# One loop of 64 attention steps over two batches, with both merges at the end, in a Branchformer forward-and-backward kernel

## The chip, the cores and the metric

The kernel runs on one core of a Trainium2 chip. The metric is the device time of one execution in microseconds. A core has a matrix engine (TensorE, in the profile PE, with its weight loads as PEld), three engines for elementwise work (VectorE: DVE, ScalarE: ACT, GpSimd: POOL) and a sequencer (SyncE: SP) that here only issues DMA transfers. Each engine works through its own queue in order; semaphores tie them together. SBUF is the core's memory of 128 partitions, PSUM the banks into which PE writes.

## The reference

The inputs are x of shape (2, 4000, 144) in bf16, weights, and grad_out of x's shape. Cut to what is computed, the forward function is

```python
xa = layernorm(x)
q, k, v = split(xa @ w_qkv, 3)
p = softmax(q @ k.T * D ** -0.5)                     # 4000 x 4000 per batch
glob = (p @ v) @ w_att_out
u, g = split(gelu(xa @ w_mlp_in), 2)
g = layernorm(g)
gc = sum(pad(g)[i:i+T] * dw_csgu[i] for i in range(5))
loc = (u * gc) @ w_mlp_out
m = concat(glob, loc)
m = m + sum(pad(m)[i:i+T] * dw_merge[i] for i in range(5))
y = x + m @ w_merge
```

and the kernel returns y together with the vector-Jacobian product for grad_out: the gradient of x and of all seven weights (nine outputs).

## The kernel before

A batch's 4000 tokens are laid out as 125 partitions of 32 tokens, token number 32 p + j in partition p, column j. So a "tile" or "block" j of the 32 is one token of each partition, 125 tokens in all (PB = 125, NB = 32). The normalised input xa_aug holds xa in this layout with a column of ones; xaT_m and R hold its transpose (128 channels and the remaining 16), XR the remaining channels stacked for four matmuls at once, goT the transposed grad_out. acc (125 x 32 x 144, f32) collects the gradient of xa for all blocks, and Yn_d, ug_d and Zn_d are DRAM tensors for per-tile results.

The attention of a batch, `phase_att` (from L1029), is a loop over the 32 query tiles with a drain behind it. The steps are software-pipelined. In step t:

- `jit_mm` and `jit_tr` (L1069, L1090) project the queries and the upstream gradients of tile t + 1 and transpose them.
- `quad` (L1107, L1113) multiplies them with all 4000 keys into PSUM tiles ps, 1000 columns each: scores S of tile t and dP of tile t - 1, four of each in a step.
- `S_min` (L1130, DVE) takes S from PSUM into Pbuf with the running minimum, `P_exp` (L1137, ACT) makes P from it, `PdP` (L1145 directly on DVE, or L1147 on ACT and L1149 on DVE) takes dP and multiplies it with P into Sbuf.
- `P_tr` (L1140) and `st_half` (L1311) have the DMA transpose P into PT and P*dP, in two halves, into ST. Both are issued by SP.
- `Y_half` (L1157) sums PT times xa_aug over the 32 blocks, `Z_half` (L1195) ST times xa_aug; the results are scaled (L1163 to L1179, L1199) and stored to Yn_d and Zn_d.
- `X_group` (L1234) sums, for three blocks of the keys, the products with Sbuf and Pbuf of the last two tiles in PSUM, and a DVE add (L1240; L1238 for the first write) brings them into acc. In each step half of the blocks are served, the even or the odd ones.

Between these, `local_units` (L421) gives the local branch, forward and backward, in small units that are dealt out evenly over the steps: over steps 2 to 30 in batch 0 and over steps 0 to 30 in batch 1.

The order of the instructions in this loop is not that of the source. `Planner.plan` (L784) takes the recorded instructions from step 2 of a batch to the end of its loop, simulates them with a table of costs per engine and DMA, and fixes an order on each engine. Outside of the loop, the Tile framework orders the instructions and the waits, buffers being shared through pools of tiles with a fixed number of slots. SP's and Pool's queues are in order in both.

Behind the loop of a batch stands its merge, the class `Merge` (L1429). `open_early` loads grad_out (go_h), the attention and local results (Yg) and the matrices VU through Pool's queue, behind a gate on the last ST; `Hmm` (L1502) forms the products H of grad_out's five shifts with those results (the gradients of the merge), 12 matmuls for each of 32 blocks; `tr_pieces` (L1420, L1425 with ACT copies L1421, L1426) transposes the results into YT and YS; `dm1` (L1559) forms Zn times xa; `out_g` (L1581, L1583, DVE add of x L1584) gives y for four blocks, eight times; `dx_a` (L1593, L1596) and `dx_b` (L1603, L1607, ACT L1608, POOL L1610) turn acc into the gradient of x. H of batch 0 is copied out of PSUM (L1546), stored to DRAM and added to that of batch 1 (L1548).

The main function (from L1800) runs: a head that prepares weights and batch 0; attention of batch 0; merge 0, with the preparation of batch 1 (`pre_pieces`, L337: layernorm statistics L361, normalisation L384, transposes L349 to L396) dealt out between its pieces; attention of batch 1, which begins with memsets and zero loads of Pbuf's and Sbuf's pads (L1047, L1048); merge 1 together with the weight gradients (`Final`, L1618 on). Both batches use the same tiles xaT_m, R, XR, goT and acc.

Of the kernel before, what the change touches and what calls it, by code (L numbers as in the profile page):

```python
# [7 lines left out]
BF = mybir.dt.bfloat16  # L8
# [297 lines left out]
def pre_tiles(k, b, S, xp, gp, sp):  # L306

    nc = k.nc
    NB = k.NB
    S.x_tp = xp.tile([PB, NB, D], BF, name="x_tp%d" % b)  # L310
    S.go_q = gp.tile([PB, NB + 6, D], BF, name="go_q%d" % b)
    ln_tiles(k, b, S, sp)
# [102 lines left out]

G2 = 2
# [3 lines left out]

def local_units(k, W, b, S, A, es, DHT, ps_w):  # L421

# [3 lines left out]
    pl = es.enter_context(tc.tile_pool(name="loc%d" % b, bufs=1, side="right", reuse_waits="tile"))  # L426
    sm = es.enter_context(tc.tile_pool(name="loc_sm%d" % b, bufs=4, side="right", reuse_waits="tile"))
# [155 lines left out]
    def dhT_unit(g):  # L583
        pt = ps_w.tile([96, 3 * G2, 128], BF, tag="w")
        dh = dhr[g % 2]
        for bi in range(G2):
            for ct in range(3):
                nc.tensor.transpose(pt[:, 3 * bi + ct, 0:PB], dh[:, bi, ct * 96:(ct + 1) * 96], W.ident[0:PB, 0:PB])
        dhT = sm.tile([96, 3 * G2, PB], BF, tag="dhT", bufs=3)
# [76 lines left out]
class Planner:  # L666
# [117 lines left out]
    def plan(self, i0, i1, window=400):  # L784
# [234 lines left out]
        self.groups, self.order, self.times = groups, order, times  # L1019
# [9 lines left out]
def phase_att(k, W, b, S, A, M, head=None):  # L1029
    nc, tc = k.nc, k.tc  # L1030
    NB, NG, T = k.NB, k.NG, k.T
    NCH = NG
# [3 lines left out]
    with ExitStack() as es:  # L1036
        ab = es.enter_context(tc.tile_pool(name="att_buf%d" % b, bufs=1, side="left", reuse_waits="tile"))
        small = es.enter_context(tc.tile_pool(name="att_small%d" % b, bufs=4, side="left", reuse_waits="tile"))
        gw = es.enter_context(tc.tile_pool(name="att_gw%d" % b, bufs=3, side="left", reuse_waits="tile"))
        ps_sg = es_sg.enter_context(tc.tile_pool(name="ps_sg%d" % b, bufs=2, space=PSUM, side="right", reuse_waits="tile"))  # L1040
        ps_yz, ps_w = k.ps_yz, k.ps_w
        Pbuf = ab.tile([128, NPB, GW], BF, name="Pbuf")
        Sbuf = ab.tile([128, NDB, GW], BF, name="Sbuf")
        def pads():
            for (buf_, nb_) in ((Pbuf, NPB), (Sbuf, NDB)):
                for n_ in range(nb_):
                    nc.gpsimd.dma_start(buf_[PB:128, n_, :], k.zdram[0:128 - PB, :])  # L1047
                nc.gpsimd.memset(buf_[0:PB, :, :].rearrange("p n (a b) -> p (n a) b", b=128)[:, :, PB:128], 0.0)  # L1048
        PT = ab.tile([128, NB, 128], BF, name="PT")
        ST = ab.tile([128, NB, 128], BF, name="ST")  # L1050
        QBs = ab.tile([PB, NPB, 2, D], BF, name="QBs")
        qbr = [ab.tile([PB, 2, D], BF, name="qb%d" % i) for i in range(3)]
        qrr = [ab.tile([PB, 256], BF, name="qr%d" % i) for i in range(3)]
        znr = [ab.tile([PB, 256], BF, name="zn%d" % i) for i in range(2)]
        def clr():
            for t_ in qrr:
                nc.gpsimd.memset(t_[:], 0.0)
            for t_ in znr:
                nc.gpsimd.memset(t_[:, D:256], 0.0)
        if head is None:  # L1060
            clr()
        xaTm, R, XR, xaa = S.xaT_m, S.R, S.XR, S.xa_aug
        QT, QB, RL, TY, YZ, ZN, ZT, NM, DHT = {}, {}, {}, {}, {}, {}, {}, {}, {}
        units, u0 = [], (0 if head is None else 2)
        if head is None:
            pads()
            units += local_units(k, W, b, S, A, es_loc, DHT, ps_w)

        def jit_mm(i):  # L1069
            ti = slice(i * PB, (i + 1) * PB)  # L1070
            pj = ps_w.tile([PB, 2 * D], F32, tag="w")
            nc.tensor.matmul(pj[:], R[:, ti], W.RW[:, 0:2 * D], start=True, stop=False)
            nc.tensor.matmul(pj[:, 0:D], xaTm[:, ti], W.Q0[:], start=False, stop=False)
            for kk in range(5):
                h = i + 4 - kk
                nc.tensor.matmul(pj[:, D:2 * D], S.goT[:, h * PB:(h + 1) * PB], W.VUT[:, kk, 0:D], start=False, stop=(kk == 4))
            qb = qbr[i % 3]
            nc.scalar.copy(qb[:], pj[:].rearrange("p (a b) -> p a b", b=D))
            QB[i] = qb
            for h in range(2):  # L1080
                rems(nc.gpsimd.tensor_copy, i, h)

        def rems(eng, i, h):


            v = qrr[i % 3][:].rearrange("p (a r c) -> p a r c", a=4, r=2)
            v = v[:, 0:4:3, :, 0:DR] if h == 0 else v[:, 1:3, :, 0:DR]
            eng(v, QB[i][:, h, 128:D].rearrange("p (a r c) -> p a r c", a=1, r=1).to_broadcast([PB, 2, 2, DR]))

        def jit_tr(i):  # L1090
            qb = QB[i]
            pt = ps_w.tile([128, 4, 128], BF, tag="w")
            for q, src in enumerate((qb[:, 0, 0:128], qrr[i % 3][:, 0:128], qrr[i % 3][:, 128:256], qb[:, 1, 0:128])):
                nc.tensor.transpose(pt[:, q, 0:PB], src, W.ident[0:PB, 0:PB])
            qt = gw.tile([128, 4, PB], BF, tag="qt")
            nc.scalar.copy(qt[:], pt[:, :, 0:PB])
            QT[i] = qt

        def pchunk(pb, c2):
            return Pbuf[0:PB, pb, c2 * 1024:(c2 + 1) * 1024]  # L1100

        def quad(work, stacked=True):


            pp = [ps_sg.tile([PB, 2, 512], F32, tag="sg", name="ps") for _ in range(len(work) // 2)]
            for r, (i, h, c) in enumerate(work):
                mm = nc.tensor.matmul(pp[r // 2][:, r % 2, 0:CH], QT[i][:, 3 * h, :], xaTm[:, c * CH:(c + 1) * CH], start=True, stop=False)  # L1107
            with tc.issue_after(mm.ins):
                for r, (i, h, c) in enumerate(work):
                    q = c % 4 if stacked else 3  # L1110
                    rs = slice(32 * q, 32 * q + DR)
                    xr = XR[rs, (c // 4) * CH:(c // 4 + 1) * CH] if stacked else R[rs, c * CH:(c + 1) * CH]
                    nc.tensor.matmul(pp[r // 2][:, r % 2, 0:CH], QT[i][rs, 1 + (q // 2 + h) % 2, :], xr, start=False, stop=True)  # L1113
            return [p[:, :, 0:CH].rearrange("p h (a b) -> p h a b", b=PB) for p in pp]

        def S_work(i, c2):
            return [(i, 0, 2 * c2), (i, 0, 2 * c2 + 1)]

        def dP_work(i, c2):
            return [(i, 1, 2 * c2), (i, 1, 2 * c2 + 1)]  # L1120

        def pv(buf, n, c2):
            return buf[0:PB, n, c2 * 1024:(c2 + 1) * 1024].rearrange("p (h a b) -> p h a b", h=2, b=128)[:, :, :, 0:PB]

        def S_min(i, c2, src):

            if c2 == 0:
                NM[i] = small.tile([PB, 5], F32, tag="nm", name="nm")
            if True:
                nc.vector.tensor_scalar(pv(Pbuf, i % NPB, c2), src, -1.0, 3.0e38, op0=ALU.mult, op1=ALU.min, accum_out=NM[i][:, c2:c2 + 1])  # L1130
            if c2 == 3:
                nc.vector.tensor_reduce(NM[i][:, 4:5], NM[i][:, 0:4], axis=AX.X, op=ALU.min)  # L1132

        def P_exp(i, c2):

            v = pv(Pbuf, i % NPB, c2)
            nc.scalar.activation(v, v, ACT.Exp, bias=NM[i][:, 4:5], scale=-1.0)  # L1137

        def P_tr(i):
            nc.sync.dma_start_transpose(out=PT[:], in_=Pbuf[:, i % NPB, :])  # L1140

        def PdP(i, c2, src, direct):

            if direct:
                nc.vector.tensor_tensor(pv(Sbuf, i % NDB, c2), src, pv(Pbuf, i % NPB, c2), op=ALU.mult)  # L1145
            else:
                nc.scalar.copy(pv(Sbuf, i % NDB, c2), src)  # L1147
                sc = Sbuf[0:PB, i % NDB, c2 * 1024:(c2 + 1) * 1024]
                nc.vector.tensor_tensor(sc, sc, pchunk(i % NPB, c2), op=ALU.mult)  # L1149

        def Y_half(i, h):
            if h == 0 and i not in YZ:
                yz = ps_yz.tile([PB, 2, 145], F32, tag="yz")
                YZ[i] = yz
            Y = YZ[i][:, 0, :]
            for j in range(16 * h, 16 * h + 16):
                nc.tensor.matmul(Y, PT[0:PB, j, 0:PB], xaa[:, j, 0:D + 1], start=(j == 0), stop=(j == NB - 1))  # L1157
# [871 lines left out]
```

## Time and profile before

| | us |
|---|---|
| time, median of 3 runs | 1391.16 |
| lowest and highest of the runs | 1387.9, 1392.22 |
| the profiled execution's own time | 1390.59 |
| its span in the trace | 1388.8 |
| first S_min of tile 3, batch 0 | 80.4 |
| first S_min of tile 31, batch 0 | 585.2 |
| first S_min of tile 0, batch 1 | 719.8 |
| first S_min of tile 2, batch 1 | 746.4 |
| first S_min of tile 31, batch 1 | 1258.5 |
| last add into acc, batch 1 | ends about 1310 |

The span is what the trace holds of one execution; the rest of the execution's own time lies around it. All times of the profile are counted from the start of the span. The times of the first S_min of a tile mark the pace of the loop: 28 steps from 80.4 to 585.2 are 18.03 us each, 29 steps from 746.4 to 1258.5 are 17.66 us each.

### The profile page before, as it was taken

How to read it: one execution, taken by the hardware profiler on the slowest of the kernel's cores; microseconds unless marked ns; L12 is line 12 of the kernel's file. 1: busy time of each engine (PE TensorE's matmuls, PEld its weight loads, DVE VectorE, ACT ScalarE, POOL GpSimd, SP SyncE). 2: the span in 40 equal slices, each digit the busy share in tenths (PEclk: the TensorE clock that was granted, in tenths of full speed). 3: DMA queues.
4: the chain of work that ended last, by engine and by line, in shares of the span. 5: the costliest groups of instructions: out<-in, count | busy, mean ns of one | idle time of the engine just before them, and what ended most of it. 6: DMA issues, size and time to landing. Idle time of an engine off the chain costs nothing.

```text
span 1388.8 us, 39713 instructions
## 1 busy us (share of the span) xinstructions
PE 1290.7 (93%) x16254; PEld 1067.0 (77%) x16254; DVE 1055.4 (76%) x2815; ACT 830.3 (60%) x1387; POOL 539.3 (39%) x1087
## 2 busy tenths in 40 slices
PE   5989999999999999989887999999999999999898
PEld 3677777778877877879765778788887787778797
DVE  6578888788887877758647888788888887877564
ACT  5856665666666666634526656666766665665271
POOL 8534333334334342256424334343443433334320
PEclk9999999999999999999999999999999999999999
DMA  4467857677767767784217677877776766767512
GB/s 118 90 121 139 145 105 126 114 132 128 121 127 130 121 119 131 111 186 121 85 44 124 127 127 130 130 130 135 126 139 123 134 125 124 142 124 148 140 43 72
DMA packets 553637, 168.59 MB, mean 121 GB/s; under 512 B 536432, under 2 KB 548354, under 8 KB 553413
## 3 DMA queue, kind: packets, MB, share of 16 engines
q1 hardware_dynamic: 547818, 153.74, 60.5%
q0 software_dynamic: 5088, 12.11, 3.4%
q8 instruction: 127, 2.08, 0.6%
q14 instruction: 56, 0.45, 0.1%
q10 hardware_dynamic: 548, 0.21, 0.1%
HBM read 21.04 MB, written 14.12 MB: 25 GB/s over the span
## 4 chain that ended last, share of the span: by engine, by line
PE 44%; DMA 7%; DVE 7%; ACT 4%; POOL 2%; issue 2%; DVEq 0%; SPq 0%; POOLq 0%; ACTq 0%
PE X L1234 10%; PE ps L1107 8%; PE yz L1195 5%; PE yz L1157 5%; DMA PT<-Pbuf 3%; PE ps L1113 3%; PE po L1581 3%; DMA go_h<-in_grad_out_dram 1%; DVE t L1607 1%; DMA ST<-Sbuf 1%; DVE Pbuf L1130 1%; ACT Pbuf L1137 1%; PE pd L564 1%; DVE acc L1240 1%; PE pc L549 1%
## 5 line engine op out<-in xcount | busy, mean ns | idle before, releaser
L1130 DVE TENSOR_SCALAR_CACHE_REDUCE Pbuf<-ps 125x1000 bf16<-125x1000 f32 x256 | 306.6, 1199 | 115.3 <-PE ps L1113 110.9
L1137 ACT ACTIVATE Pbuf<-Pbuf,nm 125x1000 bf16<-125x1000 bf16 x256 | 282.9, 1135 | 126.0 <-DVE nm L1132 125.7
L1234 PE MATMUL X<-QBs,Sbuf 125*125 125x144 bf16 x2048 | 304.3, 230 | 4.7 <-DVE acc L1240 2.8
L1234 PE MATMUL X<-QBs,Pbuf 125*125 125x144 bf16 x2048 | 300.1, 228 | 4.0 <-POOL QBs L1179 4.0
L1234 PEld LDWEIGHTS <-Sbuf 125*125 125x125 bf16 x2048 | 264.9, 139 | 20.0 <-issue 19.9
L1107 PE MATMUL ps<-xaT_m,qt 128*125 128x500 bf16 x1024 | 264.6, 377 | 9.8 <-DVE Pbuf L1130 4.1
L1147 ACT CAST Sbuf<-ps 125x1000 bf16<-125x1000 f32 x189 | 187.9, 994 | 138.4 <-PE ps L1113 137.9
L1234 PEld LDWEIGHTS <-Pbuf 125*125 125x125 bf16 x2048 | 265.6, 139 | 5.8 <-issue 5.3
L1240 DVE TENSOR_TENSOR acc<-X,acc 125x432 f32<-125x432 f32 x372 | 202.0, 551 | 54.9 <-PE X L1234 53.4
L1195 PE MATMUL yz<-xa_aug,ST 125*125 125x144 bf16 x2048 | 150.6, 229 | 20.9 <-ACT ty L1173 19.9
L1195 PEld LDWEIGHTS <-ST 125*125 125x125 bf16 x2048 | 141.5, 139 | 27.5 <-issue 26.0
L1107 PEld LDWEIGHTS <-qt 128*125 128x125 bf16 x1024 | 121.7, 137 | 52.7 <-issue 13.7
L1157 PE MATMUL yz<-xa_aug,PT 125*125 125x145 bf16 x2048 | 147.1, 230 | 8.6 <-DMA PT<-Pbuf 8.1
L1149 DVE TENSOR_TENSOR Sbuf<-Sbuf,Pbuf 125x1024 bf16<-125x1024 bf16 x189 | 133.9, 709 | 23.0 <-ACT Sbuf L1147 22.8
L1157 PEld LDWEIGHTS <-PT 125*125 125x125 bf16 x2048 | 137.8, 139 | 16.2 <-DMA PT<-Pbuf 11.9
L1113 PEld LDWEIGHTS <-qt 16*125 16x125 bf16 x1024 | 37.0, 128 | 100.5 <-issue 99.9
L1113 PE MATMUL ps<-XR,qt 16*125 16x500 bf16 x1016 | 113.8, 422 | 0.0
L1145 DVE TENSOR_TENSOR Sbuf<-ps,Pbuf 125x1000 bf16<-125x1000 f32 x67 | 80.0, 1194 | 5.2 <-PE ps L1113 4.0
L597 POOL TENSOR_TENSOR A_dwc<-l_fl,A_dwc 128x512 f32<-128x512 f32 (+2 forms) x48 | 35.6, 741 | 103.0 <-ACT l_fl L596 103.0
L1175 POOL TENSOR_SCALAR QBs<-qb,rl 125x144 bf16<-125x144 bf16 x64 | 25.4, 397 | 127.5 <-DVE rl L1163 121.2
L1209 ACT COPY zt<-pt 128x250 bf16<-128x250 bf16 x64 | 23.7, 371 | 69.3 <-PE pt L1207 69.1
L574 POOL TENSOR_SCALAR l_w<-gd,nc,c 125x144 f32<-125x144 bf16 x64 | 30.6, 486 | 85.5 <-DVE nm L1132 44.7
(557 smaller groups left out, 2557.4 us busy)
## 6 DMA issues: line engine op xcount, KB each, us to landing
Yn_d<-yn SPq DMA_DIRECT2D x64, 35.2 KB
Zn_d<-zn SPq DMA_DIRECT2D x64, 35.2 KB
ug_d<-ugr SPq DMA_DIRECT2D x32, 70.3 KB
xo<-in_x_dram SPq DMA_DIRECT2D x16, 140.6 KB
out_dram<-dxo SPq DMA_DIRECT2D x16, 140.6 KB
go_h<-in_grad_out_dram POOLq DMA_DIRECT2D x4, 504.0 KB, 7.1
Zn<-Zn_d SPq DMA_DIRECT2D x4, 504.0 KB
ST<-Sbuf SPq DMA_TRANSPOSE x124
```

Source lines behind the costliest of these rows:

```text
L1107: mm = nc.tensor.matmul(pp[r // 2][:, r % 2, 0:CH], QT[i][:, 3 * h, :], xaTm[:, c * CH:(c + 1) * CH], start=True, stop=False)
L1113: nc.tensor.matmul(pp[r // 2][:, r % 2, 0:CH], QT[i][rs, 1 + (q // 2 + h) % 2, :], xr, start=False, stop=True)
L1130: nc.vector.tensor_scalar(pv(Pbuf, i % NPB, c2), src, -1.0, 3.0e38, op0=ALU.mult, op1=ALU.min, accum_out=NM[i][:, c2:c2 + 1])
L1137: nc.scalar.activation(v, v, ACT.Exp, bias=NM[i][:, 4:5], scale=-1.0)
L1145: nc.vector.tensor_tensor(pv(Sbuf, i % NDB, c2), src, pv(Pbuf, i % NPB, c2), op=ALU.mult)
L1147: nc.scalar.copy(pv(Sbuf, i % NDB, c2), src)
L1149: nc.vector.tensor_tensor(sc, sc, pchunk(i % NPB, c2), op=ALU.mult)
L1157: nc.tensor.matmul(Y, PT[0:PB, j, 0:PB], xaa[:, j, 0:D + 1], start=(j == 0), stop=(j == NB - 1))
L1195: nc.tensor.matmul(Z, ST[0:PB, j, 0:PB], xaa[:, j, 0:D], start=(j == 0), stop=(j == NB - 1))
L1234: nc.tensor.matmul(X[:, jj, :], l, r, start=(n_ == 0), stop=(n_ == len(ops) - 1))
L1240: nc.vector.tensor_tensor(av, X[:, 0:nj, :], av, op=ALU.add)
L1581: nc.tensor.matmul(po[:, q, :], YT[h][:, (i + kk) * PB:(i + kk + 1) * PB], VU[h][:, kk, :], start=(n_ == 0), stop=False)
```

## The change

The loop of `phase_att` runs over s = 0 to 64 for both batches; tile s belongs to batch s // 32. Pipelining goes on across the seam: in step 32, S is of batch 1's first tile and dP of batch 0's last. The planner now takes everything from step 2 to behind the drain as one piece. Local units of batch 0 are dealt out over steps 2 to 27, those of batch 1 over steps 34 to 61.

Batch 1 gets tiles of its own for xa_aug, xaT_m, R, XR and goT; acc stays one tile. In steps 28 to 31 the new function `prep_late` prepares batch 1, in 30 pieces that are dealt out evenly: x and grad_out come in four groups of 8 tokens, each in one buffer, on SP's queue.

```diff
+def prep_late(k, W, b, S, es, pst):
...
+    def load(Q, v, n, g):
+        if g < 4:
+            Q[g] = sp.tile([PB, 8, D], BF, tag=n, name=n, bufs=1)
+            load_tok(k, Q[g], 0, v, 8 * g, 8 * g + 8, nc.sync)
...
+    def stats(g):
+        for j in range(8):
+            nc.vector.bn_stats(st[:, 8 * g + j, :], XQ[g][:, j, :])
...
+    def norm(g):
...
+        for j in range(8 * g, 8 * g + 8):
+            eng = nc.vector if j % 2 else nc.gpsimd
+            eng.tensor_scalar(S.xa_aug[:, j, 0:D], XQ[g][:, j % 8, :], S.rstd_x[:, j:j + 1], nmr[:, j:j + 1], op0=ALU.mult, op1=ALU.add)
...
+    P = [lambda: (start(), load(XQ, xv, "xq", 0), load(GQ, gv, "gq", 0)), halos]
+    for g in range(4):
+        P += [lambda g=g: stats(g), lambda g=g: gr(g), lambda g=g: (norm(g), load(XQ, xv, "xq", g + 1)), lambda g=g: (gm(2 + 8 * g, GQ[g][:]), load(GQ, gv, "gq", g + 1))]
+        if g:
+            P += [lambda g=g: gs(g - 1)]
+        P += [lambda g=g: xam(g), lambda g=g: xar(g)]
```

Here `gm` and `xam` are eight PE transposes with an ACT copy (goT, xaT_m), `gs` and `xar` eight with a DVE copy (R), `xar` with two small DMAs to XR, `gr` a Pool copy.

The local units' tiles of batch 1 need the place of batch 0's tiles, and acc is needed for batch 1, so what merge 0 still needs of batch 0 is stored to DRAM from within the loop, by SP, and read back behind the drain:

```diff
+        st_half(1)
+        if s == 6:
+            k.spill_xa0()
+        if s in (NB + 1, NB + 2):
+            k.spill_acc0(s - NB - 1)
...
+    k.spill_xa0 = lambda: nc.sync.dma_start(k.xa_d[:], SS[0].xa_aug[:, :, 0:D])
+    k.spill_acc0 = lambda q: nc.sync.dma_start(k.acc_d[:, q:NB:2, :], acc[:, q:NB:2, :])
...
     def open_late(self):
...
+        S.acc = m0.tile([PB, NB, D], F32, name="acc0")
+        S.xa_aug = m0.tile([PB, NB, XW], BF, name="xa0r")
+        for g in range(4):
+            sl = slice(8 * g, 8 * g + 8)
+            k.nc.sync.dma_start(S.acc[:, sl, :], k.acc_d[:, sl, :])
+            k.nc.sync.dma_start(S.xa_aug[:, sl, 0:D], k.xa_d[:, sl, :])
+        self.load_z(0)
+        self.load_go(1)
```

`open_late` takes the place of the attention's tiles, which are closed before it. `X_group` copies into acc at the first write of a block of a batch and adds from then on. `late`, in step 62, loads go_h and Yg of batch 0 and VU through Pool's queue, without the gate; `load_go(1)`, `load_src(1)` and `load_z(1)` later load the same of batch 1.

Behind the drain, both merges follow each other. H is summed over both batches in PSUM (`Hmm(n)` with n up to 63), and `hb` reads it from there; its copy, store, reload and addition go. x for `out_g` is loaded two to four groups ahead in four buffers.

```diff
+    phase_att(k, W, SS, A, head, 28, 2 * NB - 2, prep, dict(late=M.late, drain=drain))
+    k.es_att.close()
     M.open_late()
...
+    side = [lambda g=g: M.dx_a(0, g) for g in range(k.NG)]
+    for q, f in enumerate(M.tr_pieces(0)):
         f()
         M.fill(1)
         if side and q >= 2:
...
+    M.load_src(1)
+    M.dm1(0)
+    M.load_z(1)
+    xo = [M.load_x(0, 0), M.load_x(0, 1)]
     for g in range(k.NG):
...
+        if g + 2 < k.NG:
+            xo.append(M.load_x(0, g + 2))
+        M.out_g(0, g, xo[g])
+        M.dx_b(0, g)
+    M.es_m0.close()
...
+    side = [F.dwc, F.dwi, F.weights] + [lambda g=g: M.dx_a(1, g) for g in range(k.NG)]
+    for q, f in enumerate(M.tr_pieces(1)):
         f()
+        M.fill(1, 2 * NB)
         if side and q % 2 == 1:
             side.pop(0)()
+    M.fill(NB, 2 * NB)
+    F.hb(M.H)
...
+    M.dm1(1)
+    M.out_g(1, 0, xo[0])
```

What is behind it is as before, with dx_b(1, ·) for dx_b and out_g(1, ·) for out_g.

More of the change, by code (lines that the diff above doesn't have):

```diff
@@ L1018, in plan @@
                 now = ev[0]
-        self.groups, self.order, self.times = groups, order, times
+        self.groups, self.order, self.times, self.preds, self.ready = groups, order, times, preds, ready
         for e in E:
@@ new lines, in P_exp, with P_tr, PdP @@
+    def P_exp(i, c2):
+        v = pv(Pbuf, i % NPB, c2)
+        nc.scalar.activation(v, v, ACT.Exp, bias=NM[i][:, 4:5], scale=-1.0)
+    def P_tr(i):
+        nc.sync.dma_start_transpose(out=PT[:], in_=Pbuf[:, i % NPB, :])
+    def PdP(i, c2, src, direct):
+        if direct:
+            nc.vector.tensor_tensor(pv(Sbuf, i % NDB, c2), src, pv(Pbuf, i % NPB, c2), op=ALU.mult)
+        else:
+            nc.scalar.copy(pv(Sbuf, i % NDB, c2), src)
+            sc = Sbuf[0:PB, i % NDB, c2 * 1024:(c2 + 1) * 1024]
+            nc.vector.tensor_tensor(sc, sc, pchunk(i % NPB, c2), op=ALU.mult)
@@ new lines, in X_group @@
+    def X_group(b, tiles, blocks):
+        S = SS[b]
+        nj = len(blocks)
+        X = ps_w.tile([PB, 3, D], F32, tag="w")
+        for jj, j in enumerate(blocks):
+            zt = ZT[b].pop(j, None)
+            ops = []
+            for i in tiles:
+                ops.append((Sbuf[0:PB, i % NDB, j * 128:j * 128 + PB], QBs[:, i % NPB, 0, :]))
+                ops.append((Pbuf[0:PB, i % NPB, j * 128:j * 128 + PB], QBs[:, i % NPB, 1, :]))
+            if zt is not None:
+                ops += [(zt[:, q, :], W.M1T[:, q, :]) for q in range(2)]
+            for ct, a in enumerate(DHT[b].pop(j, [])):
+                ops.append((a, W.WiT[:, ct, :]))
+            for n_, (l, r) in enumerate(ops):
+                nc.tensor.matmul(X[:, jj, :], l, r, start=(n_ == 0), stop=(n_ == len(ops) - 1))
+        av = S.acc[:, blocks[0]:blocks[-1] + 1:2, :]
+        if blocks[0] not in seen[b]:
+            seen[b].update(blocks)
+            nc.vector.tensor_copy(av, X[:, 0:nj, :])
+        else:
+            nc.vector.tensor_tensor(av, X[:, 0:nj, :], av, op=ALU.add)
@@ new lines, in phase_att @@
+    es_sg.close()
+    M = hooks["drain"]()
+    xg = X_groups(NT + 1)
+    for c2 in range(2, 4):
+        last_tr(Pbuf[:, (NT - 1) % NPB, :], PT, c2)
+    for h in range(2):
+        Y_half(NT - 1, h)
+    zt_tr(NT - 2)
+    for c2 in range(4):
+        last_tr(Sbuf[:, (NT - 1) % NDB, :], ST, c2)
+    M.fill(2)
+    for h in range(2):
+        Z_half(NT - 1, h)
+    for _ in range(5):
+        X_group(*xg.pop(0))
+    M.fill(4)
+    X_group(*xg.pop(0))
+    zt_tr(NT - 1)
+    for g_ in X_groups(NT + 2):
+        X_group(*g_)
@@ L1414, in transposes @@
+    X_group(1, [], [NB - 1])
+    assert not any(ZT) and not any(DHT) and done == len(units)
+    k.PL.plan(i0, k.PL.mark())
 def transposes(k, W, tok, rem, dstm, dsts, j0, n, engs):
```

984 lines of the change are left out of this document (486 added, 498 removed).

## The prediction

> **What bounds the kernel now.** I read the page's busy table and slices first, then busy time by window, then the chain of waits, then groups of instructions.
>
> ```profile
> span 1388.8 us, 39713 instructions
> ...
> PE 1290.7 (93%) x16254; PEld 1067.0 (77%) x16254; DVE 1055.4 (76%) x2815; ACT 830.3 (60%) x1387; POOL 539.3 (39%) x1087
> ...
> PE   5989999999999999989887999999999999999898
> ...
> DMA  4467857677767767784217677877776766767512
> ```
>
> PE is nearly full except at the start, in the middle and at the end; the granted clock is 0.93 to 1.00 in the windows that follow. The windows cut the span where it changes character; the columns are PE, PEld, DVE, ACT, POOL busy, granted clock, share of 16 DMA engines, GB/s.
>
> ```profile
> 60.00:580.00 520.00, 498.06 (x6230) 407.27 (x6229) 417.62 (x1054) 330.17 (x535) 188.83 (x380) 0.99 0.71 125
> 585.20:746.40 161.20, 133.62 (x1775) 118.74 (x1776) 104.38 (x322) 74.20 (x118) 75.48 (x132) 0.93 0.45 108
> 746.40:1258.50 512.10, 494.93 (x6232) 404.18 (x6232) 413.91 (x1041) 328.10 (x529) 192.09 (x388) 1.00 0.73 130
> 1258.50:1310.00 51.50, 45.60 (x605) 41.24 (x604) 28.41 (x57) 16.12 (x25) 23.44 (x49) 0.93 0.60 137
> 1310.00:1342.00 32.00, 31.49 (x481) 29.28 (x479) 24.19 (x125) 26.09 (x48) 6.92 (x12) 1.00 0.30 89
> 1342.00:1388.80 46.80, 39.19 (x544) 34.73 (x541) 25.95 (x100) 14.99 (x44) 5.57 (x5) 0.96 0.24 68
> ```
>
> The loops are the first and third row: PE busy 96 and 97%, DVE 80%. The second row goes from the first S_min (L1130) of batch 0's last tile to that of batch 1's tile 2: drain, Merge 0 with batch 1's preparation, and the refill. Its chain of waits has
>
> ```profile
> 598.18 4.23 DMA ST<-Sbuf
> ...
> 607.96 10.45 DMA go_h<-in_grad_out_dram
> ```
>
> so the seam holds a load of 10 us that nothing covers, and then a pipeline that starts empty. PE is without work for 161.2 - 133.6 = 28 us of it.
>
> **The change part by part.** I count to the start of S_min of the last tile (T), to the last add into acc (D), and to the end. Before, T is 1258.5 (third row's edge), D 1310, the end 1388.8.
>
> *Removed: the seam.* Merge 0 leaves the middle, and so do the drain, the refill and the second pads. What remains of the 161.2 us are three steps. A step without local work is PE-bound: S and dP (264.6 + 113.8 us of L1107 and L1113 over 64 tiles) 5.9, X 64 matmuls at 0.75 per 12 (chain rows) 4.0, Y and Z 64 at 1.16 per 16 (chain rows) 4.6, the next tile's projections about 1: 15.5 us. Saving 161.2 - 46.5 = 115.
>
> *Moved: local units and preparation.* Batch 0's 29 steps from tile 3 (80.4) to 31 (585.2) take 18.03 us each, so a step's local work is about 2.5, some 75 per batch. Squeezed into 26 steps it is the same PE work, no cost. Batch 1's window before began at tile 2 and held 29 of 31 units of local work; now all 31 lie behind it: +5. The preparation goes into steps 28 to 31 (see prep_late): on DVE 32 bn_stats at 0.30, 16 normalisations at 0.30 (L361, L384), 8 copies into R at 0.68 (L357, L396), small ones, about 23 us; PE about 7. A bare step has on DVE four S_min 1.2, one direct PdP 1.2, three PdP 0.71, six adds 0.55, and 1.5 of small ones: about 13. With 5.8 more DVE needs 18.8 in those four steps, where PE would need 17.3: DVE becomes the bound there, and three of the four lie before tile 31, where PE would have won 2.5 each from the missing local work. Together about +10 (bounds: 0 if it fits the old 18.03; +24 if in addition each of the eight 8-token loads, in single buffers on SP, holds the transposes queued behind it for 3 us, the 3.2 us of x_tp_n being the nearest row). So T = 1258.5 - 115 + 5 + 10 = 1158.5.
>
> *Added: three spills on SP.* xa_aug0 (4000 pieces of 288 B, 1.15 MB) in step 6 and two halves of acc (2000 pieces of 576 B, 1.15 MB each) in steps 33 and 34, each queued behind the second ST transpose, so ahead of the next PT transpose, on which Y waits. What a copy of 125 partitions gets shows where nothing else flows (first and last row below); the middle rows are loads cut into 112 + 13 partitions:
>
> ```profile
> 700.00:710.00 10.00, 10.00 (x167) 10.00 (x165) 4.85 (x9) 2.17 (x3) 0.00 (x0) 1.00 0.28 78
> 612.00:622.00 10.00, 6.47 (x103) 6.15 (x101) 2.44 (x7) 2.80 (x5) 5.44 (x11) 1.00 0.86 211
> 1278.00:1288.00 10.00, 9.57 (x139) 8.63 (x138) 6.95 (x15) 3.86 (x7) 6.05 (x13) 1.00 0.96 238
> 1370.00:1387.00 17.00, 12.50 (x170) 10.90 (x169) 8.36 (x40) 2.08 (x9) 0.00 (x0) 0.95 0.28 76
> ```
>
> 0.28 of 16 is 4.5 engines, 76 to 78 GB/s. A spill then takes 1.15 MB / 77 = 15 us. P_tr follows it by some 7 us, so PT lands up to 8 late. PT normally comes just in time:
>
> ```profile
> L1140 SPq DMA_TRANSPOSE PT<-Pbuf x62: 4722/4860/6213, 39.5 to 1259.9; - x62
> ...
>   PEld L1157: 11.9, 14
> ```
>
> It already holds PE 14 times in 62, so there is little slack. The acc spills add a second wait: batch 1's first copies into the same rows stand in DVE's queue ahead of the next S_min, which PE needs to free ps. I take 6 us per spill, 18. Bounds: 0 (each hidden, or at 225 GB/s done in 5) and 45 (all serial).
>
> [...]
>
> *Moved: merge 0 to the end.* From D before, 78.8 us follow. Added to them is merge 0's PE work: H (L1502) 32 blocks 24, transposes 7.5, dm1 4, out_g (L1581, L1583; 16 x 2 x 12 matmuls at 0.063) 24: 60 us, less 2 for an H eviction that goes (L1546, L1548): 137 if nothing waits. But acc0 (2.30 MB) and xa0 (1.15 MB) are read back first, into the attention's own tiles, so not before D: all copies of 125 partitions on SP, 3.46 MB / 75 = 46 us, with start and Zn 51. Behind them stand, in the new program's fixed order: on PE dm1(0), which needs all of xa0 and Zn, ahead of out_g(0); on DVE the dx_a(0) and dx_b(0) groups with all of dx_a(1) between them, and only then the first add of out_g(0) (now L1684) that frees its PSUM; on ACT dx_b(0)'s activations between the last ten evictions of YT and YS, so these wait for the reload too; on Pool load_src(1), which waits for H(0) and is covered (needed 70 us later; 10 if it weren't). By
>
> ```profile
> L1607 DVE SCALAR_TENSOR_TENSOR t<-xa_aug,dx_s,acc 125x144 f32<-125x144 bf16 x32 | 13.0, 465 | 1.2 <-POOL dxo L1610 1.2
> L1593 DVE TENSOR_REDUCE dx_s<-acc 125x4 f32<-125x576 f32 x8 | 5.9, 742 | 0.0
> ```
>
> what is left for DVE after the last landing is about 8 x (0.74 + 4 x 0.25) for dx_a(1) and 8 x (0.16 + 4 x 0.3) for dx_b(0), 25 us. So the first add comes at D + 76, while PE has 36 us to do till then: 40 idle. Then 20 of out_g(0), the 32 of H and transposes of batch 1 (fifth row) and the 46.8 of the sixth: D + 174. Bounds: 137 (nothing waits) and 185 (xa0's 288 B pieces at the lower 68 GB/s and the o_ stores behind them).
>
> *Drain* 51.5, as the fourth row; it now lies in the plan, and go_h, Yg and VU loads were there before too (0.60 DMA share): no change, bounds -5 and +8.
>
> *Sum:* 1158.5 + 18 + 51.5 + 174 = 1402 of span; the profiled execution took 1390.59 for a span of 1388.8, so +1.8: 1403.8, and that execution stands 0.6 under the median of 1391.16. I predict 1404. In short: 100 us (115 less 5 and 10) come out ahead of T, 95 come back behind D, where PE idles instead, and the price of parking acc and xa decides.
>
> **Rivals.** *The copies are fast.* If the chip spreads them over 16 engines (225 GB/s as in the 112-partition rows), the reload takes 15 us, the last piece lands at D + 19, the first add comes at D + 44 against 36 of PE work, and the end is D + 145; spills of 5 us pass within the slack of the plan (2). Then 1158.5 + 2 + 51.5 + 145 + 1.8 = 1359. It speaks for it that the shares were seen on x and out copies alone, against it that both such windows show the same 4.5 engines. It decides the sign where the reload falls under about 37 us.
>
> *The spills hide, the reload does not.* Spills lie in stretches with 0.7 DMA share and P_tr is issued one step ahead; if PT is late only by what the planner's distance absorbs, 18 becomes 3: 1389, no change. Against it: Y's 14 waits on PT.
>
> *The preparation spoils four steps and its loads the transposes.* T + 14, and spills at 24: 1424. For: DVE needs 18.8 there, single buffers on an in-order SP queue, loads that wait for DVE's norm. Against: the static order places each piece in a free slot.
>
> *Only the idle moves:* the seam's gain smaller (the bare steps at 18, +8) with half the spill cost is 1403 as well, indistinguishable by time, but visible in the steps' pace.
>
> **How the numbers follow.** My forecast with the terms above has 0.45, the bad preparation 0.17, hidden spills 0.15, fast copies 0.15, the rest mixes. A measurement of this kernel can tell about 0.3%, 4.2 us. Slower: 0.61 (forecast, bad preparation). Same: 0.13 (most of hidden spills). Faster: 0.26 (fast copies, and mixes of a shorter end with hidden spills). The range reaches to the fast copies partly and past the bad preparation: 1366 to 1430; the forecast's own is 1392 to 1418.
>
> **What would show it.** After the seam: S_min of tiles 31 to 34 in steps of 15 to 19 us, no gap. Spills: PE idle of 5 to 8 us on PT in steps 7, 34, 35, and DMA share near 0.3 in the reload, 45 to 50 us long, with PE idle about 40 behind the first out_g. It is wrong if the reload takes under 30 us, if DVE gets to out_g's adds before D + 60, or if the steps with preparation run past 22 us.

## The result, and the profile after

| | before | after |
|---|---|---|
| time, median | 1391.61 us (4 runs, 1387.9 to 1392.22) | 1467.08 us (4 runs, 1464.0 to 1470.83) |
| profiled span | 1388.8 us | 1466.7 us |
| S_min of the last tile starts (T) | 1258.5 | 1239.2 |
| last add into acc ends (D) | 1310.7 | 1283.6 |
| from D to the end | 78.1 | 183.1 |

The changed kernel is slower, by a ratio of 1.0549 (95% interval 1.0516 to 1.0583). The forecast was 1404 with a range to 1430. The sign is right, the size far off: 76 us instead of 13.

The page of the changed kernel, its span, busy times and three of its slice rows (PE, granted clock, DMA):

```profile
span 1466.7 us, 39541 instructions
...
PE 1301.0 (89%) x16190; PEld 1076.3 (73%) x16190; DVE 1052.9 (72%) x2808; ACT 829.6 (57%) x1384; POOL 516.4 (35%) x1045
...
PE   5897899999999998887799999989999984957698
...
PEclk9999899999999999998899999999999997978899
DMA  3466776667676668577576687666677787145302
```

PE's work is the same (1301 us busy against 1291), the span 78 us longer. The deep dip of the DMA row in the middle (4 2 1 before) is gone with merge 0, but PE's digits there are no better than before (8 8 8 7 7 against 8 9 8 8 7), and PE is thin in new places: one early slice and much of the last quarter. The granted clock is below full in or next to these places as well. The windows of the same kernel, cut where the steps change (columns as before: PE, PEld, DVE, ACT, POOL busy, granted clock, DMA share, GB/s):

```profile
548.90:642.40 93.50, 79.06 (x904) 64.04 (x905) 67.62 (x185) 47.22 (x65) 29.39 (x60) 0.93 0.68 127
642.40:672.90 30.50, 29.42 (x352) 23.09 (x351) 23.49 (x49) 17.30 (x27) 5.79 (x15) 1.00 0.78 137
672.90:729.90 57.00, 38.18 (x389) 29.53 (x390) 31.60 (x78) 22.52 (x37) 14.11 (x30) 0.82 0.68 125
729.90:1193.40 463.50, 451.88 (x5751) 370.84 (x5750) 381.54 (x968) 302.43 (x492) 183.89 (x366) 1.00 0.72 128
1193.40:1239.20 45.80, 19.96 (x200) 16.75 (x201) 12.09 (x25) 8.97 (x12) 17.83 (x38) 0.70 0.93 166
1239.20:1283.60 44.40, 41.02 (x583) 36.79 (x582) 28.82 (x58) 15.49 (x21) 4.83 (x12) 1.00 0.19 39
1283.60:1382.20 98.60, 65.76 (x879) 64.37 (x877) 59.74 (x248) 41.64 (x79) 30.46 (x44) 0.81 0.49 140
1382.20:1466.70 84.50, 76.76 (x1098) 70.11 (x1095) 24.09 (x101) 30.89 (x65) 3.93 (x3) 0.97 0.14 40
```

Read from the top: four steps with the preparation, 93.5 us, some 23 each; the two steps across the seam, 15 us each with PE 96% busy, as hoped; two steps with the acc spills, 28 and 29 us; 26 steps of the loop, PE busy 97% as before; one step, from tile 62 to 63, of 45.8 us with PE busy for 20; the drain; merge 0, with PE idle for a third of it; and the rest. The waits view of the same kernel (who waited for what: us in total, times, longest) names the releasers:

```profile
PEld L1288 <- DMA ST<-Sbuf: 23.3, 4, 12.9
...
PEld L1191 <- POOL qr L1185: 20.2, 1, 20.2
...
PEld L1250 <- DMA PT<-Pbuf: 19.5, 18, 5.9
...
DVE dx_s L1693 <- DMA acc<-acc_d: 16.8, 4, 9.9
...
DVE acc L1336 <- DMA acc_d<-acc: 10.1, 1, 10.1
```

Four of these five have a long wait at one of the new transfers: a transposition (ST) behind a spill, Pool's qr copy in the step to tile 63, the reload, and the first copy into acc behind its spill. The waits for PT are many and short, as before (11.9 us in 14 waits there). In the profile before, PE's waits for ST came to about 1 us.

### The profile page after: what moved, and what is told of

Its sections match the earlier page's. It is cut to its first block, busy times and chain, and to the rows that moved or that the text cites. A ratio compares the mean times of both kernels' runs of the same rounds, so it can differ in the third digit from the quotient of the medians.

```text
span 1466.7 us, 39541 instructions
## 1 busy us (share of the span) xinstructions
PE 1301.0 (89%) x16190; PEld 1076.3 (73%) x16190; DVE 1052.9 (72%) x2808; ACT 829.6 (57%) x1384; POOL 516.4 (35%) x1045
## 5 line engine op out<-in xcount | busy, mean ns | idle before, releaser
L1332 PEld LDWEIGHTS <-Sbuf 125*125 125x125 bf16 x2048 | 266.0, 139 | 14.4 <-issue 14.2
L1338 DVE TENSOR_TENSOR acc<-X,acc 125x432 f32<-125x432 f32 (+1 forms) x373 | 202.8, 551 | 72.1 <-PE X L1332 69.4
L1202 PEld LDWEIGHTS <-qt 128*125 128x125 bf16 x1024 | 122.4, 137 | 54.1 <-issue 16.1
L1237 DVE TENSOR_TENSOR Sbuf<-ps,Pbuf 125x1000 bf16<-125x1000 f32 x66 | 78.8, 1194 | 6.0 <-PE ps L1209 3.8
L1681 PE MATMUL po<-VUl,YT 128*125 128x144 bf16 x640 | 55.1, 234 | 12.5 <-DVE o__22788 L1684 6.2
L1681 PEld LDWEIGHTS <-YT 128*125 128x125 bf16 x640 | 52.9, 143 | 14.4 <-issue 13.5
```

The source lines that it names most:

```text
L1332: nc.tensor.matmul(X[:, jj, :], l, r, start=(n_ == 0), stop=(n_ == len(ops) - 1))
L1338: nc.vector.tensor_tensor(av, X[:, 0:nj, :], av, op=ALU.add)
L1681: nc.tensor.matmul(po[:, q, :], YT[h][:, (i + kk) * PB:(i + kk + 1) * PB], VU[h][:, kk, :], start=(n_ == 0), stop=False)
```

## Experiments

The first group takes one suspect each. Times are medians beside runs of the kernel before on the same chip (1390 to 1392 us in all groups); single steps and stages are from the profiled executions. Steps are named by the tile whose S_min ends the interval, one more than the loop's own s: the preparation of s = 28 to 31 lies in steps 29 to 32, the late loads of s = 62 in step 63. Step 63 scatters: in kernels that leave it alone it took 37.4 to 45.7 us, and 45.7 is that of the changed kernel itself. A time that falls by up to 8 us can be this alone, so single steps and stages are given beside the times.

**The spills, cut into 112 + 13 partitions.**

```diff
-    k.spill_acc0 = lambda q: nc.sync.dma_start(k.acc_d[:, q:NB:2, :], acc[:, q:NB:2, :])
+    cut = (slice(0, 112), slice(112, PB))
+    k.spill_acc0 = lambda q: [nc.sync.dma_start(k.acc_d[p, q:NB:2, :], acc[p, q:NB:2, :]) for p in cut]
```

and `spill_xa0` likewise.

> The changed kernel, but each of the three spills on SP is cut into 112 + 13 partitions. Theory (a spill of 125 partitions runs on 4.5 engines for 13 to 18 us, and the transposes behind it on SP and DVE's first copies into acc wait that long): with some 12 to 16 engines a spill takes 5 us, steps 7, 35 and 36 fall from 30.8, 28.0 and 29.0 us to about 19 each, the time to about 1435. Rival (the wait is for the order of SP's queue or for the hazard on acc as such, not for the rate): the steps lose less than 4 us each, the time stays above 1455.

Measured: 1435.8 us; steps 7, 35 and 36 took 20.1, 20.0 and 19.9 us instead of 30.8, 28.0 and 29.0, so 27.8 of the 31 us are just there. In the timeline of SP in the changed kernel, the ST half that the planner put right behind the first and the second spill takes 18.0 and 13.2 us, and PE stands 12.8 and 8.9 us for it. The first spill (a line of SP's timeline and one of PE's), then the second (SP's):

```profile
131.50 18.02 SPq L1408 DMA_TRANSPOSE ST<-Sbuf  x1
...
151.65 1.60 PE L1288 MATMUL yz<-xa_aug,ST 125*125 125x144 bf16 x11 [12.79 <-DMA ST<-Sbuf]
...
669.64 0.85 SPq L1950 DMA_DIRECT2D acc_d<-acc  x1
670.67 13.21 SPq L1408 DMA_TRANSPOSE ST<-Sbuf  x1
```

In the same kernel, DVE's first copy into acc behind the third spill (the second half of acc) waits 10 us, with S_min behind it; PE stands 7.9 us of that time:

```profile
714.24 0.61 DVE L1336 COPY acc<-X 125x432 f32<-125x432 f32 x1 [10.09 <-DMA acc_d<-acc]
714.76 1.19 DVE L1224 TENSOR_SCALAR_CACHE_REDUCE Pbuf<-ps 125x1000 bf16<-125x1000 f32 x1
```

With the cut (SP of that kernel), the first half of acc goes out as two transfers and the transposition behind them takes 5 us:

```profile
656.38 2.46 SPq L1951 DMA_DIRECT2D acc_d<-acc  x2
658.96 5.00 SPq L1408 DMA_TRANSPOSE ST<-Sbuf  x1
```

The rate was the cause. Of the two waits that the prediction named, DVE's for acc is there; the other is a wait for ST and not, as predicted, for PT.

**The spills on ACT's queue**, still of 125 partitions (`nc.scalar.dma_start` for `nc.sync.dma_start` in both).

> The changed kernel, but the three spills, still of 125 partitions, are issued by ACT and so stand in ACT's DMA queue and not in SP's. Theory A (each DMA engine serves a queue in order, so only the transposes behind a spill on the same queue wait for it): the ST and PT transposes pass, step 7 falls from 30.8 to under 22 us; steps 35 and 36 keep what DVE's first copies into acc wait for, since the read still takes 13 to 18 us: 21 to 25 us; time 1440 to 1450. Theory B (the few DMA engines are shared, whatever the queue): all three steps stay above 25 us, time above 1458.

Measured: 1449.3 us; steps 7, 35 and 36 took 23.5, 24.1 and 31.6 us. Their sum falls by 8.6 us; 8 more of the 18 us are the scatter of step 63. So neither theory holds alone: the time is within A's range, but step 7 misses its 22 us and step 36 is even longer than before. SP's timeline in that kernel shows the transpositions slowed but not held:

```profile
127.43 11.16 SPq L1408 DMA_TRANSPOSE ST<-Sbuf  x2
138.65 0.47 SPq L1264 DMA_DIRECT2D Yn_d<-yn  x1
139.29 9.21 SPq L1233 DMA_TRANSPOSE PT<-Pbuf  x1
```

The two ST halves take 11.2 us together there (one takes 1.9 in the middle and 4.0 at most in the kernel before) and PT 9.2 (4.9 in the middle before): slowed beside the spill, but no longer behind all of it. DVE's wait for acc stays, 11.8 us. One ST half behind the spill on the same queue took 18.0 us, two beside it on another queue 11.2 together. Copies of 125 partitions had a DMA share of 0.28, 4.5 of 16 engines, in the first and last window of the prediction's table of copies, and 0.44, at 68 GB/s, from 140 to 147 us in the first spill of the changed kernel; the two windows with cut copies have 0.86 and 0.96, and the gain of the cut here agrees. What sets the number of engines of a transfer was not shown.

**The reload, cut the same way.**

```diff
-            k.nc.sync.dma_start(S.acc[:, sl, :], k.acc_d[:, sl, :])
-            k.nc.sync.dma_start(S.xa_aug[:, sl, 0:D], k.xa_d[:, sl, :])
+            for p in (slice(0, 112), slice(112, PB)):
+                k.nc.sync.dma_start(S.acc[p, sl, :], k.acc_d[p, sl, :])
+                k.nc.sync.dma_start(S.xa_aug[p, sl, 0:D], k.xa_d[p, sl, :])
```

> The changed kernel, but the reload of acc and xa behind the drain is cut into 112 + 13 partitions. Theory (the 40 us reload sets when the adds of out_g(0) come, 66 us behind the last add into acc): the reload takes about 16 us, the first add of out_g(0) comes 25 us earlier, the time is about 1445. Rival (DVE's own order, reduces and dx groups of both batches ahead of the first add, and ACT's and Pool's part of dx_b set it): the first add moves by less than 10 us and the time by less.

Measured: 1443.0 us, 24 less than the changed kernel; 19.0 of these are between D and the end (183.1 to 164.1), and step 63, which the edit does not touch, was 8 us shorter. The first add of out_g(0) came 66 us behind D in the changed kernel and 40 us behind it with the cut (D 1277.5 there), as DVE's timelines of the two show:

```profile
1349.67 0.82 DVE L1684 TENSOR_TENSOR o__22443<-po,xo 125x288 bf16<-125x288 f32 x2
```

```profile
1317.91 0.45 DVE L1685 TENSOR_TENSOR o__22451<-po,xo 125x288 bf16<-125x288 f32 x1
```

So the adds move by 26 us and the end by 19: the reload sets the start of out_g(0).

**The preparation over eight steps** (24 for 28 in the call of `phase_att`, so that batch 0's local units end with step 23).

> The changed kernel, but the preparation of batch 1 is dealt out over steps 24 to 31 and batch 0's local units over steps 2 to 23. Theory (too much DVE work in four steps: 5.8 us in each beyond the 13 of a bare step): halved per step it fits beside the PE work, and of the some 24 us that steps 28 to 31 lose nearly all come back, less what the denser local steps lose: the time falls by 12 to 22 us. Rival (each piece costs its own wait in an in-order queue, load to statistics to Pool to transpose, and the clock that halves behind a long wait): the loss stays with the 30 pieces however far they are spread, and the time changes by less than 6 us.

Measured: 1445.5 us; S_min of tile 32 came at 625.4 instead of 642.4. The last four of the steps in this kernel's windows, to be held against the row from 548.9 to 642.4 above:

```profile
557.40:625.40 68.00, 61.73 (x760) 48.94 (x759) 54.12 (x127) 36.51 (x49) 15.36 (x34) 1.00 0.80 138
```

68.0 us with DVE busy for 54.1 and the clock at 1.00, where with all of the preparation in them it was 93.5 us, 67.6 and 0.93. The steps before, from tile 3 on, lose 11.0 in return, so spreading brings 14.5 us; most of the rest of the 22 us is step 63, 8 us shorter. Crowding was the larger part of the cost, not the pieces as such.

**The preparation's copies into R on ACT instead of DVE** (`nc.scalar.copy` for `nc.vector.tensor_copy` in `gs` and `xar`), four steps as before.

> The changed kernel, but the eight copies of the preparation into R (0.68 us each) go to ACT, which is busy for 47 of the 93.5 us of steps 28 to 31, instead of DVE; still four steps. Theory (DVE's amount of work makes these steps long): 5.5 us less on DVE shorten the four steps by about 5 us, from 93.5 to 88 or 89, and the time by as much. Rival (waits between engines and queues that do not fit into so few steps, load to statistics to Pool to transposes, and the halved clock behind them): the four steps change by less than 2 us or grow.

Measured: 1455.5 us; steps 29 to 32 together 84.0 us. Kernels with the same preparation took 89.8 to 93.5 there, so the gain is 6 to 9 us for 5.5 us less on DVE: each microsecond taken from DVE shortens these steps by at least as much. Step 63 was 7 us shorter as well, and the start of the kernel 5 us longer, both untouched by the edit. DVE's amount of work is not all of it, since DVE is busy for only 67.6 of the 93.5 us. The waits view of the changed kernel, in the window of these four steps, names waits from engine to engine within the preparation:

```profile
PEld L492 <- POOL xa_aug L464: 7.5, 12, 2.8
...
DVE pnm L461 <- POOL rstd_x L457: 4.9, 4, 1.6
```

How much of the time such waits cost by themselves is not separated here.

**The copies behind the late loads.** In `late`, the Pool copies go_r and both Yr wait for loads, and the qr copy of the last tile stands behind them on Pool, as its timeline in the changed kernel shows:

```profile
1206.15 0.67 POOL L1572 COPY go_r<-go_h 125x576 bf16<-125x576 bf16 x1 [8.18 <-DMA go_h<-in_grad_out_dram]
...
1216.74 0.67 POOL L1588 COPY Yr<-Yg 125x576 bf16<-125x576 bf16 x1 [1.85 <-DMA Yg<-Yn_d]
1229.38 0.67 POOL L1588 COPY Yr<-Yg 125x576 bf16<-125x576 bf16 x1 [11.97 <-DMA Yg<-ug_d]
...
1232.17 0.25 POOL L1185 COPY qr<-qb 125x64 bf16<-125x64 bf16 x1
```

The edit moves the three copies into two functions, which are called in the drain.

```diff
     def drain():
         M.open_h()
+        M.rem_go(0)
+        M.rem_src(0)
         return M
```

> The changed kernel, but the three Pool copies that need the landed loads of step 62 (go_r, both Yr) are issued in the drain instead of right behind the loads; the 20 loads themselves stay in step 62. Theory (the copies hold Pool's queue until the loads land, and the qr copy of the last tile, for which PE waits 20 us, stands behind them): step 62 to 63 falls from 45.7 us to about 20 to 24, the time from 1467 to about 1440 to 1445. Rival (the loads themselves: 20 descriptor issues of 0.55 us on Pool and their traffic against the transposes): the step stays above 35 us, the time above 1455.

Measured: 1467.8 us, step 63 at 44.4 us: no gain, the rival's case. In that kernel the issues of the loads themselves wait on Pool, so qr comes only 7 us earlier, and SP's transpositions are slow (Pool's lines, then SP's, then PE's wait in this step):

```profile
1205.89 0.56 POOL L1586 DMA_DIRECT2D Yg<-ug_d  x1 [3.49 <-DMA go_h<-in_grad_out_dram]
...
1223.83 0.56 POOL L1560 DMA_DIRECT2D VUl<-VU_d  x1 [8.94 <-DMA Yg<-ug_d]
...
1224.96 0.41 POOL L1185 COPY qr<-qb 125x64 bf16<-125x64 bf16 x2
```

```profile
1198.83 13.49 SPq L1408 DMA_TRANSPOSE ST<-Sbuf  x1
...
1213.47 14.82 SPq L1408 DMA_TRANSPOSE ST<-Sbuf  x1
```

```profile
PEld L1288 <- DMA ST<-Sbuf: 19.8, 1, 19.8
```

An ST half, 2.0 us in the median of the changed kernel, takes 13.5 and 14.8; PE waited 19.8 us for it instead of 20.2 for qr.

**The late loads behind the gate again**, at the end of step 63, as the kernel before had them.

```diff
-                hooks["late"](ST)
...
+        if s == NT - 1:
+            hooks["late"](ST)
...
+        gate = pr.tile([1, 1], BF, name="gate")
+        g_ = nc.gpsimd.tensor_copy(gate[:], ST[0:1, NB - 1, 0:1])
+        with k.PL.issue_after(g_.ins):
...
```

> The changed kernel, but the late loads of batch 0 (go_h, Yg, VU, 3.8 MB through Pool's queue) are issued at the end of step 63 behind a Pool copy that reads the last ST, as the kernel before had it, instead of in step 62. Theory (it is the traffic of these loads that holds the transposes of the last two steps, and Pool's queue behind them): step 62 to 63 falls from 45.7 to 17 to 20 us; the drain grows by 5 to 12 us, since H(0) waits for the loads there; the time is about 1445 to 1452. Rival (the stall only moves, since the drain has nothing else to do while the loads come): the drain grows by over 20 us and the time stays above 1460.

Measured: 1457.6 us (its profiled execution, 1451.6, was the shortest of four). Step 63 and the drain in this kernel's windows:

```profile
1190.10:1204.80 14.70, 14.70 (x182) 11.68 (x182) 11.69 (x24) 6.46 (x10) 3.67 (x9) 1.00 0.75 134
1204.80:1266.90 62.10, 44.55 (x598) 40.45 (x598) 28.76 (x58) 17.36 (x24) 19.31 (x42) 0.86 0.52 119
```

Step 63 falls by 31 us to 14.7, with PE never idle; the drain grows from 44.4 to 62.0, more than the theory and less than the rival gave, and the time too lies between the two. So the loads, where they stood, were the cause of the long step: through the copies on Pool's queue in the changed kernel, through the slow transpositions in the run before this one. More than half of the gain went into a new wait in the drain (PE 14.1 us for QBs).

**Four edits together**: gate, both cuts, eight steps.

> The changed kernel with four edits together: late loads behind the gate, spills and reload cut into 112 + 13 partitions, preparation over eight steps. If the causes are separate, the gains add: 31 (spills) + 24 (reload) + 22 (preparation) + 15 to 22 (late loads), from 1467 to about 1368 to 1376, under the 1392 of the kernel before. If they cover each other (a stall taken away in one place comes back in the next), the time stays above 1390.

Measured: 1393.7 us, ratio to the kernel before 1.000 (0.998 to 1.002): no difference from it. The single gains in time (31, 24, 22 and 10 off 1467) would give 13 us less, but two of them (reload and preparation) hold 8 us each from the scatter of step 63, a step that the gate shortens as well. Counted by the stages that each edit touches, in the profiled executions, the gains are 27.8 (spills' steps), 19.0 (D to the end), 14.5 (tile 3 to tile 32) and 13.4 (31.0 in step 63 less 17.6 in the drain). Taken off the span of 1466.7 that gives 1392, and the span measured is 1392.8, closer than single executions warrant: so counted they add, and what comes back in the next place is the gate's 17.6 alone. T is at 1168.5, but the drain still takes 61.7 us. In it PE stands 14 us for QBs, which is behind the copies on Pool (timeline of that kernel):

```profile
1207.17 0.67 POOL L1591 COPY Yr<-Yg 125x576 bf16<-125x576 bf16 x1 [1.79 <-DMA Yg<-Yn_d]
1211.62 0.67 POOL L1591 COPY Yr<-Yg 125x576 bf16<-125x576 bf16 x1 [3.78 <-DMA Yg<-ug_d]
...
1214.46 0.40 POOL L1268 TENSOR_SCALAR QBs<-qb,rl 125x144 bf16<-125x144 bf16 x1
```

**Besides, the copies behind QBs** (`rem_go(0)` and `rem_src(0)` ahead of `M.fill(2)` in the drain).

> The four edits together, and besides the three Pool copies that need the landed loads (go_r, both Yr) come in the drain behind the scaling of the last tile's QBs. In the four edits together PE waits 14.2 us in the drain for QBs (L1268), which stands behind these copies on Pool. Theory (the copies, and not the 20 loads themselves, hold QBs): most of the gap goes, the drain falls from 61.7 to about 50 us, the time from 1394 to about 1382 to 1386. Rival (the wait only moves to H(0), which needs the same loads): the drain stays above 57 us, the time above 1389.

Measured: 1382.5 us, ratio 0.9939 (0.9918 to 0.9960), the drain 48.7 us. Much the same edit that brought nothing while the loads ran beside the last transpositions brings 11 us once they come behind them.

**Besides, four buffers for o_ and dxo** (`bufs=4`).

> As the run before it with the copies moved, and the output tiles o_ and dxo have four buffers instead of two. Theory (in the end, DVE's adds and Pool's dxo wait for stores of 125 partitions to leave their buffers, some 7 us at the first out_g and 2 us at each dxo, while PE waits for the adds): the end falls from 162 to about 150 us, the time by 8 to 12 more. Rival (the chain of t, activation and dxo over DVE, ACT and Pool sets the pace whatever the stores do): the time falls by less than 4.

Measured: 1378.4 us, ratio 0.9897 (0.9868 to 0.9926); from D to the end 161.4 us, against 168.8 in the run before, whose profiled execution was 5 us above its median, and 162.5 in the four edits together. The gain of 4 us in time lies between the two expectations, and the stages do not show surely that it comes from the end; most of the end is not held by the stores. Windows of this kernel, the last four steps with the preparation, the rest of the loop, the drain and the end:

```profile
546.70:615.90 69.20, 63.14 (x761) 49.87 (x759) 54.14 (x127) 36.56 (x49) 15.37 (x34) 0.98 0.79 136
615.90:1166.30 550.40, 532.09 (x6679) 434.45 (x6680) 449.57 (x1118) 350.70 (x568) 207.82 (x419) 1.00 0.74 132
1166.30:1217.00 50.70, 40.01 (x519) 35.54 (x520) 28.88 (x58) 17.35 (x24) 19.35 (x42) 0.90 0.67 145
1217.00:1378.40 161.40, 142.98 (x2055) 135.43 (x2052) 80.47 (x348) 71.07 (x143) 34.68 (x47) 0.94 0.41 107
```

PE is busy 91% in the four steps and 97% behind them, so the loop is full across the seam. The largest gaps for their length are now the drain's 10.7 us and some 18 us of the end.

**Besides, the stores cut too** (112 + 13).

> As the run with four buffers, and the stores of o_ and dxo are cut into 112 + 13 partitions too. Theory (SP's queue is held by stores that run on 4.5 engines): another 3 to 8 us less. Rival (four buffers already hide the stores; twice the number of issues on SP costs 0.3 us each): within 3 us of the run before, or slower.

Measured: 1377.9 us, ratio 0.9900 (0.9872 to 0.9928): the same.

**The store edits in the kernel before.**

> The kernel before with the same two edits of the stores (four buffers for o_ and dxo, stores cut into 112 + 13), to see what of a gain is not due to the order of the merges. Theory (before, its end and its middle are set by PE and by the loads): within 4 us of 1392. Rival (the stores hold it as well): 5 to 10 us less.

Measured: 1392.9 us, ratio 1.0008 (0.9986 to 1.0030): nothing. The mended version is 0.6% below the kernel before without the store edits and 1% with them, and these edits alone bring nothing there. So the gain needs the new order with its mended transfers; which part of the change gives it (the one loop, H kept in PSUM, x loaded ahead) is not separated.

## Why the prediction was wrong

*The seam's gain was right.* The two bare steps took 14.2 and 16.4 us (15.5 forecast). With the faults mended, the preparation spread over eight steps among them, T is at 1166 to 1169, some 90 us before the old 1258.5, and the cut spills still cost 6 to 7 us of that time. The net of removal, denser local units and preparation was put at 100 us.

*The late loads are the step that failed.* The prediction put the drain at "no change" because "go_h, Yg and VU loads were there before too", and nothing for the steps ahead of it. They were, but behind a gate on the last ST; the changed kernel issues them a step earlier, beside the last transpositions. That the gate goes stands in the description of the change and was not priced. The step to tile 63 took 45.7 us where some 17.7 were forecast, +28 (+20 to +27 in the other kernels with the loads in this place), and 14.7 us with the gate back. The DMA share in this window is 0.93, against 0.72 in the loop.

*The preparation was mis-sized.* +10 was forecast with 24 as the bad end; by the prediction's own rows four steps of 18.8 instead of 15.5 would have been +13, so the fourth step was left out of the sum. Steps 29 to 32 took 93.5 us instead of 4 times 18.8: +18 on top, and past the 22 us a step that the prediction named as a sign of being wrong. The sum of DVE's durations was not too small (67.6 us busy, 75 forecast), but it was taken as the length of the steps. DVE alone was not the bound: it was idle for 26 of the 93.5 us, in a chain of work over SP, DVE, Pool and PE. That spreading the work brings 14.5 us, and 5.5 us less of DVE 6 to 9 us, shows that the density was most of it.

*The spills were right in rate, wrong in one of their waits, and half in size.* Steps 7, 35 and 36 exceed 17.7 by 34.7 us together, 18 were forecast, 45 was the bound. The ST halves behind the first two took 18.0 and 13.2 us (15 forecast for a spill). But the sum had PT waiting, with 7 us of lead; the planner put the second ST half right behind these two spills, without any lead, and PE stood 12.8 and 8.9 us for it. At the third spill it was DVE's copy into acc, as predicted, 10.1 us.

*Drain and end nearly cancel.* The drain took 44.4 us instead of 51.5, the end 183.1 instead of 174 (within its bounds of 137 and 185). Within the end the mechanism was as predicted: the reload took 40 us (46 forecast, 51 with its start and Zn), and the first add came 26 us behind its last landing (25 forecast), at D + 66 instead of D + 76. Out_g(0) was done at D + 98.6 (96 forecast), so the 10 us gained were lost again in its own 32 us (20 forecast), and the last two parts took 84.5 where 78.8 were forecast.

The terms, added to the forecast span of 1402: +28 late loads, +18 preparation, +17 spills, +3 at the start (tile 3 came at 83.1 instead of 80.4), -3 as what is left for the rest of the loop (-6, were the fourth step of the preparation in the forecast), -7 drain, +9 end give 1467, as measured. Two slips in the prediction changed nothing: its "29 steps" from tile 3 to 31 are 28 (18.03 us each is right), and by the sum that gives D + 174, the fast copies' D + 145 would be 143.

*The rivals.* "The preparation spoils four steps and its loads the transposes" was the closest and too small, 1424. No run shows its 24 us for the spills, 8 at each in a wait for PT: the longest of PE's 18 waits for PT in the changed kernel was 5.9 us, and the three steps exceeded 17.7 by 34.7 us together. "The copies are fast" failed in its premise, but the cuts show what it would have been worth: 28 us in the spills' steps and 19 in the end. "The spills hide" is refuted by the steps.

## What to carry to other kernels

A transfer that moves into a full pipeline is priced by the queue and the engines that it now shares, not by whether it was there before; where the old kernel has a gate in front of a load, ask what the load would disturb without it. A move that pays on the busiest engine can be lost in what it brings along: here 90 us came out of the loop, and crowded preparation, parked data and load traffic took them until the transfers were cut (in the kernel before, a DMA share of 0.86 and 0.96 with cut copies and 0.28 with those of 125 partitions), the preparation was spread and the gate put back. And gains are best added up by the stage that each edit touches, with what comes back in the next stage: here such a sum met the four edits together, while the sum of the times was 13 us off.

## What the runs showed of the hardware

The stall of step 63 cost PE more than its length. Windows of the changed kernel around the stall of step 63 and in the reload:

```profile
1212.00:1232.00 20.00, 0.49 (x8) 0.30 (x6) 1.48 (x4) 4.18 (x4) 5.59 (x11) 0.61 1.19 173
1232.00:1236.00 4.00, 3.52 (x30) 3.52 (x31) 0.71 (x2) 0.58 (x1) 1.98 (x6) 0.50 0.42 128
1236.00:1244.00 8.00, 8.00 (x95) 6.42 (x95) 6.18 (x12) 2.26 (x3) 0.00 (x0) 0.95 0.01 2
...
1300.00:1316.00 16.00, 5.34 (x45) 5.02 (x45) 7.99 (x44) 4.66 (x7) 0.00 (x0) 0.50 0.35 115
```

The DMA share of 1.19 counts packet times that overlap. PE had no work from 1212.5 to 1232.5 us. The granted clock was 1.00 from 1212 to 1216, 0.55 to 1220 and 0.50 from there to 1236, so that PE worked at 0.50 for the 4 us behind the stall; it was 0.89 from 1236 to 1240 and 1.00 in the 4 us behind that. In the reload, where PE's work comes in small portions with waits between, the clock stays at 0.50 for 16 us: eight transpositions take 1.00 us there, and 0.60 from 1284 to 1296 at a clock of 1.00.

Two more were not expected. In the run with the three copies moved to the drain, issues on Pool waited themselves for earlier transfers of Pool's to land (3.49 and 8.94 us above), so that the loads held Pool's queue there without any copy behind them. And transpositions were slow beside Pool's loads: ST halves took 13.5 and 14.8 us in that run (2.0 in the median of the changed kernel), and in the changed kernel a PT took 11.7, with a median of 4.9.
